# Grouped-query attention over a KV cache: K and P transposed in 32x32 word blocks on VectorE, V loaded by 16 KB rows, q and P as block-diagonal weights of four heads

## The chip, the cores and the metric

One core of a Trainium2 chip runs the kernel. The metric is the device time of one execution in microseconds, the median of several. The span in a profile (first to last instruction) is about 1.9 us shorter than that time. PE is TensorE (PEld its weight loads), DVE is VectorE, ACT is ScalarE, POOL is GpSimd, SP issues the DMAs. A number after PV, V or K is the batch (0 to 31). The trace holds 16 landing events for each load (a load is one DMA); "landed" below means the last of them, and all times are us from the start of the span.

## The reference, cut to what matters

```python
B, Sq, D = 32, 4, 1024
Hq, Hkv, Sk, Dh = 32, 4, 2048, 128          # all bfloat16
q = (x @ wq)                                # [32 batches, 4 tokens, 32 heads, 128]
k = repeat(k_cache, 8); v = repeat(v_cache, 8)
scores = einsum("bhqd,bhkd->bhqk", q, k) * Dh ** -0.5
o = einsum("bhqk,bhkd->bhqd", softmax(scores), v)
return o @ wo
```

Each batch has 2 MB of K and 2 MB of V: 134.2 MB in all. wq and wo are 8.4 MB each. A batch's 4 KV heads (the groups g) serve 8 query heads of 4 tokens each, so 32 rows of scores per group and 128 per batch. "QK" below is the scores, "PV" the product of the probabilities P with V, and the "projection" is the product with wo at the end.

## The kernel before

Each operation is recorded with the names of what it waits for, and each engine has a list of its own. In each turn of the loop the kernel computes the scores of batch i, transposes K of batch i+1, and does PV for batch i-2. K comes by rows of 16 KB (64 tokens of 256 bytes), V by rows of 4 KB:

```python
R = 32; T = Sk // R; C = 4; TV = T // C; TT = TV // 2; NKB = 3; NVB = 3
WO = (8, 8, 8, 5, 2, 1)                     # heads of wo in each load
def load_k(b):                              # 64 tokens to a partition: 16 KB rows
    ... K_sb[:, b % NKB, :, :], k_cache[b].rearrange("g (r t) d -> (g r) t d", r=R) ...
def load_v(b):                              # 16 tokens of each group to a partition: 4 KB rows
    src = v_cache[b].rearrange("g (p t) d -> p g (t d)", p=128)
    dst = V_sb[:, b % NVB, :, :, :].rearrange("p g t d -> p g (t d)")
```

K and P are transposed on TensorE as 32-bit words (two bfloat16 each) into PSUM and copied out by DVE and ACT. QK and PV use parts of the array, each group in its own columns:

```python
def pe_fill(b, f):                          # 8 times a batch, 4 transposes each
    ... e.transpose(buf..., words(K_sb[:, b % NKB, t:t + 2, :]...), identf[:, :]) ...
def pv_mm(buf, i, g, t, waits, done):       # 64 times a batch
    ... e.matmul(buf[32 * g:32 * (g + 1), 0:Dh], lhsT=pt(i, t, g), rhs=V_sb[:, i % NVB, g, t, :],
                 start=(t == 0), stop=(t == TV - 1), tile_position=(0, 32 * g)) ...
```

After the loop come the last PVs and the projection (`oproj`): 32 heads, two matmuls of 512 columns each, waiting for each chunk of wo and for the output of the last batch.

## Time and profile before

| | before |
|---|---|
| time, median | 379.7 us |
| span | 377.8 us |
| DMA rate, 4 to 24 us (16 KB rows only) | 430 GB/s |
| DMA rate, 100 to 300 us (K by 16 KB, V by 4 KB rows) | 417 GB/s |
| PE / DVE / ACT / POOL busy | 70 / 56 / 45 / 0 % |

From the page of the kernel before: the busy share of each engine, the DMA share in tenths and the GB/s in 40 slices of 9.4 us, the chain of waits that ended last (by engine), and three groups (line, engine, operation, tiles, shapes, count, busy us and mean ns of one, idle before and its cause).

```profile
PE 264.8 (70%) x4553; PEld 190.7 (50%) x3953; DVE 213.0 (56%) x299; ACT 169.9 (45%) x266; POOL 1.3 (0%) x9
...
DMA  8999999999999999999999999999999999999982
GB/s 333 427 434 427 414 409 417 416 417 418 419 423 419 415 421 418 416 414 419 415 416 418 416 416 418 418 419 419 417 418 416 414 419 414 413 405 375 373 331 80
...
DMA 70%; PE 15%; DVE 5%; ACT 5%; SPq 3%; issue 1%
...
L264 PE MATMUL ps_r<-identf,K_sb 128*128 128x128 f32 x1024 | 122.9, 277 | 44.1 <-DMA K_sb<-in_k_cache_dram 41.3
L317 PE MATMUL ps_r<-V_sb,PT_sb 128*32 128x128 bf16 x2048 | 35.5, 222 | 44.6 <-DMA V_sb<-in_v_cache_dram 40.6
L355 ACT ACTIVATE P_sb<-ps_s,negmx 128x2048 bf16<-128x2048 f32 x32 | 63.3, 1979 | 7.0 <-DVE negmx L351 7.0
```

The DMA line is full from start to end, no engine is, and what PE waits for is K and V. The slices step from 427 to 434 GB/s (wq and K) down to about 417 once V joins. The DMA view of two stretches of the same run says it in one number each (packets, MB, rate, and how many packets are small): the first stretch is 4 to 24 us, the second 100 to 300 us.

```profile
DMA packets 589, 8.60 MB, mean 430 GB/s; under 512 B 64, under 2 KB 64, under 8 KB 64
...
DMA packets 13326, 83.43 MB, mean 417 GB/s; under 512 B 632, under 2 KB 632, under 8 KB 10767
```

The end of the timeline before (start us, duration us, engine, line, operation) shows a short tail behind the last V:

```profile
344.60 1.08 PE L317 MATMUL ps_r<-V_sb,PT_sb 128*32 128x128 bf16 x64 [1.48 <-DMA V_sb<-in_v_cache_dram]
...
350.30 1.90 PE L317 MATMUL ps_r<-V_sb,PT_sb 128*32 128x128 bf16 x64 [3.84 <-DMA V_sb<-in_v_cache_dram]
...
356.86 0.65 PE L368 MATMUL ps_s<-w_sb,QT_sb 128*128 128x512 bf16 x1 [3.90 <-DMA w_sb<-in_wo_dram]
```

PV takes 1.08 us where the granted clock was 1.00 (V 30, at 344.6 us) and 1.90 us where it was 0.50 (V 31), and starts the moment its V lands: V 31 at 350.3 us. The projection begins soon after and then waits for wo.

### The profile page before, as it was taken

To read this page: it belongs to the slowest core of one execution; us is meant where nothing else is said; L and a number is where in the kernel's file an instruction comes from. 1 tells how busy PE (TensorE), PEld (TensorE's weight loads), DVE (VectorE), ACT (ScalarE), POOL (GpSimd) and SP (SyncE) were. 2 spreads that over 40 slices of the span, in tenths; PEclk is the share of its full clock that TensorE was granted. 3 is DMA by queue.
4 is the path that set the end of the run, shared out by engine and by line. 5 is a ranking of instruction groups with operands and counts; after the bars stand their busy time and mean duration, and the time that the engine had idled before them with its cause. 6 is when DMAs were issued, how large, how long until landed. Compare 5 with 4: busy or idle time off the path is not lost.

```text
span 377.8 us, 9230 instructions
## 1 busy us (share of the span) xinstructions
PE 264.8 (70%) x4553; PEld 190.7 (50%) x3953; DVE 213.0 (56%) x299; ACT 169.9 (45%) x266; POOL 1.3 (0%) x9
## 2 busy tenths in 40 slices
PE   1889888887777666777656677766667666663476
PEld 0018656665557555555535555555545555542222
DVE  0026886777664666666656666666666666661000
ACT  1025565555555555544435554555544444444100
POOL 1000000000000000000000000000000000000000
PEclk9999999999998999999999999999999999999599
DMA  8999999999999999999999999999999999999982
GB/s 333 427 434 427 414 409 417 416 417 418 419 423 419 415 421 418 416 414 419 415 416 418 416 416 418 418 419 419 417 418 416 414 419 414 413 405 375 373 331 80
DMA packets 26774, 152.11 MB, mean 403 GB/s; under 512 B 1264, under 2 KB 1520, under 8 KB 22128
## 3 DMA queue, kind: packets, MB, share of 16 engines
q1 hardware_dynamic: 26592, 151.39, 98.2%
q8 instruction: 33, 0.54, 0.6%
q10 hardware_dynamic: 144, 0.13, 0.1%
q14 instruction: 5, 0.04, 0.0%
HBM read 151.26 MB, written 0.26 MB: 401 GB/s over the span
## 4 chain that ended last, share of the span: by engine, by line
DMA 70%; PE 15%; DVE 5%; ACT 5%; SPq 3%; issue 1%
DMA V_sb<-in_v_cache_dram 52%; DMA K_sb<-in_k_cache_dram 7%; DMA w_sb<-in_wo_dram 6%; DMA w_sb<-in_wq_dram 5%; DVE mx L350 4%; ACT P_sb L355 4%; PE ps_r L317 3%; PE ps_r L282 3%; SPq L175 3%; PE ps_r L264 2%; PE ps_s L16 2%; PE ps_s L308 2%; PE ps_s L237 1%; PE ps_s L368 1%; ACT KT_sb L276 1%
## 5 line engine op out<-in xcount | busy, mean ns | idle before, releaser
L264 PE MATMUL ps_r<-identf,K_sb 128*128 128x128 f32 x1024 | 122.9, 277 | 44.1 <-DMA K_sb<-in_k_cache_dram 41.3
L264 PEld LDWEIGHTS ps_r<-identf,K_sb 128*128 128x128 f32 x1024 | 112.7, 142 | 52.2 <-DMA K_sb<-in_k_cache_dram 44.6
L274 DVE COPY KT_sb<-ps_r 128x512 f32<-128x512 f32 x128 | 84.9, 688 | 30.9 <-PE ps_r L264 30.0
L276 ACT COPY KT_sb<-ps_r 128x512 f32<-128x512 f32 x128 | 69.6, 599 | 48.1 <-PE ps_r L264 48.1
L289 DVE COPY PT_sb<-ps_r 128x512 f32<-128x512 f32 x64 | 41.3, 687 | 65.2 <-PE ps_r L282 65.2
L350 DVE TENSOR_REDUCE mx<-ps_s 128x1 f32<-128x2048 f32 x32 | 73.3, 2292 | 7.0 <-PE ps_s L16 7.0
L317 PE MATMUL ps_r<-V_sb,PT_sb 128*32 128x128 bf16 x2048 | 35.5, 222 | 44.6 <-DMA V_sb<-in_v_cache_dram 40.6
L355 ACT ACTIVATE P_sb<-ps_s,negmx 128x2048 bf16<-128x2048 f32 x32 | 63.3, 1979 | 7.0 <-DVE negmx L351 7.0
L317 PEld LDWEIGHTS ps_r<-V_sb,PT_sb 128*32 128x32 bf16 x2048 | 30.4, 98 | 51.4 <-ACT KT_sb L276 43.1
L344 ACT ACTIVATE QT_sb<-ps_r 128x128 bf16<-128x128 bf16 x32 | 23.7, 739 | 55.0 <-PE ps_r L340 55.0
L282 PE MATMUL ps_r<-identf,P_sb 128*128 128x128 f32 x256 | 34.9, 279 | 2.6 <-ACT KT_sb L276 1.4
L334 ACT ACTIVATE o_sb<-ps_r,rinv 128x128 bf16<-128x128 f32 x32 | 11.8, 368 | 48.2 <-PE ps_r L317 48.2
L282 PEld LDWEIGHTS ps_r<-identf,P_sb 128*128 128x128 f32 x256 | 27.4, 141 | 6.3 <-ACT KT_sb L276 1.9
L308 PE MATMUL ps_s<-KT_sb,QT_sb 64*32 64x512 bf16 x512 | 26.5, 390 | 0.9 <-DVE KT_sb L274 0.9
L16 PE MATMUL ps_s<-KT_sb,QT_sb 64*32 64x512 bf16 x512 | 26.1, 383 | 0.0
L376 DVE CAST y_sb<-ps_s 128x512 bf16<-128x512 f32 x1 | 0.7, 692 | 30.5 <-PE ps_s L368 30.5
L368 PE MATMUL ps_s<-w_sb,QT_sb 128*128 128x512 bf16 x32 | 13.1, 409 | 5.9 <-DMA w_sb<-in_wo_dram 5.9
L340 PEld LDWEIGHTS ps_r<-ident,o_sb 128*128 128x128 bf16 x32 | 3.1, 96 | 20.9 <-issue 20.1
L368 PEld LDWEIGHTS ps_s<-w_sb,QT_sb 128*128 128x128 bf16 x32 | 4.9, 154 | 16.3 <-issue 8.4
L16 PE MATMUL ps_s<-w_sb,QT_sb 128*128 128x512 bf16 x32 | 12.9, 403 | 0.0
L223 DVE CAST KT_sb<-ps_r 128x512 bf16<-128x512 f32 x2 | 1.3, 687 | 20.1 <-PE ps_r L209 20.1
L308 PEld LDWEIGHTS ps_s<-KT_sb,QT_sb 64*32 64x32 bf16 x512 | 7.4, 90 | 10.4 <-issue 5.2
(28 smaller groups left out, 66.0 us busy)
## 6 DMA issues: line engine op xcount, KB each, us to landing
K_sb<-in_k_cache_dram SPq DMA_DIRECT2D x32, 2048.0 KB, 26.3
V_sb<-in_v_cache_dram SPq DMA_DIRECT2D x32, 2048.0 KB, 27.4
w_sb<-in_wq_dram SPq DMA_DIRECT2D x4, 2048.0 KB, 14.0
w_sb<-in_wo_dram SPq DMA_DIRECT2D x2, 2048.0 KB, 22.9
w_sb<-in_wo_dram SPq DMA_DIRECT2D x1, 1792.0 KB, 20.0
w_sb<-in_wo_dram SPq DMA_DIRECT2D x1, 1280.0 KB, 18.6
w_sb<-in_wo_dram SPq DMA_DIRECT2D x1, 512.0 KB, 14.9
P_sb<-in_x_dram SPq DMA_DIRECT2D x1, 256.0 KB, 2.7
```

The lines of the kernel that those rows point to most:

```text
L16: return eng.add_instruction(mybir.InstMatmult(name=nc.get_next_instruction_name(), engine=eng.engine, start_tensor_calc=start, stop_tenso ...
L264: p.op("pe", lambda e, c=c, t=t: e.transpose(buf.rearrange("p (n c) -> p n c", c=C)[:, :, c], words(K_sb[:, b % NKB, t:t + 2, :].rearrange ...
L274: p.op("dve", lambda e: e.tensor_copy(dst, buf), waits, ("kt", b, f))
L276: p.op("act", lambda e: e.copy(dst, buf), waits, ("kt", b, f))
L282: p.op("pe", lambda e, q=q: e.transpose(buf[:, q * 128:(q + 1) * 128], words(P_sb[:, (4 * f + q) * 256:(4 * f + q + 1) * 256]), identf[:, :]),
L289: p.op("dve", lambda e: e.tensor_copy(dst, buf), [("ptf", i, f)] + ([("pv", i - 2)] if i > 1 else []), ("pt", i, f))
L308: mm = lambda e, a=(out, lhsT, rhs), w=w, pos=(DW * par, 32 * g): e.matmul(a[0], lhsT=a[1], rhs=a[2], start=(w == 0), stop=(w == 1), tile_ ...
L317: p.op("pe", lambda e: e.matmul(buf[32 * g:32 * (g + 1), 0:Dh], lhsT=pt(i, t, g), rhs=V_sb[:, i % NVB, g, t, :], start=(t == 0), stop=(t = ...
L344: p.op("act", lambda e: e.activation(oT_sb[:, i * Sq:(i + 1) * Sq, 0:Hq].rearrange("p s h -> p h s"), buf[:, 0:128].rearrange("p (h s) -> ...
L350: p.op("dve", lambda e: e.tensor_reduce(mx[:, i % 4:i % 4 + 1], ps_s[:, :], AX.X, ALU.max), [("qk", i)], ("mx", i))
L355: p.op("act", lambda e: e.activation(P_sb[:, :].rearrange("p (n a) -> p n a", a=2), ps_s[:, :].rearrange("p (a n) -> p n a", a=2), ACT.Exp ...
L368: mm = lambda e, a=(out, lhsT, rhs), h=h: e.matmul(a[0], lhsT=a[1], rhs=a[2], start=(h == 0), stop=(h == Hq - 1), skip_group_check=True)
```

## The change

The intent is a DMA stream of 16 KB rows only, and fewer operations on TensorE. K and V are both laid out with 64 tokens of one group on each partition, so V's rows are 16 KB too. DVE transposes K and P directly in SBUF, in blocks of 32x32 words. Partition 32g+r then belongs to group g alone. So q and P are written into block-diagonal weights (group g's 32 partitions and 32 columns, zeros elsewhere), and one matmul over the full array does all four groups. GpSimd writes the blocks. Eight slots of 2 MB hold K, V, wq and wo in turn. The core of the diff:

```diff
-        src = v_cache[b].rearrange("g (p t) d -> p g (t d)", p=128)
+        src = (k_cache if kind == "k" else v_cache)[b].rearrange("g (r t) d -> (g r) t d", r=R)
+        p.dma("sp", lambda e, s=s, src=src: e.dma_start(big[:, s, :, :], src), waits, (kind, b), f"s_b{s}")
...
-    WO = (8, 8, 8, 5, 2, 1)
+    WO = (4, 4, 4, 4, 4, 4, 4, 2, 1, 1)
...
+        def kt(i, chunks):                       # four a batch, 128x1024 words each
+            ... p.op("dve", lambda e, s=src, d=dst: e.transpose(d, s), waits, ("kt", i, c))
+        def pt(i):
+            p.op("dve", lambda e: e.transpose(dst, src), [("exp", i)] + ([("pd", i - 2)] if i > 1 else []), ("pt", i))
+        def pd(i):                               # P into the diagonal: one buffer, PD_sb
+            for g in range(G):
+                src = words(PT_sb[rows, i % 2, :, :, :]...)
+                dst = words(PD_sb[rows, :, g, :, :]...)
+                p.op("pool", lambda e, s=src, d=dst: e.tensor_copy(d, s),
+                     (["pd0", ("pt", i)] + ([("pv", i - 1)] if i else [])) if g == 0 else [], ...)
+        def pe_pv(i):
+            for t in range(T):                   # 64 matmuls of the full array
+                ... e.matmul(buf[:, 0:Dh], lhsT=PD_sb[:, t // 2, :, :, t % 2]..., rhs=big[:, slot_of["v", i], t, :],
+                             start=(t == 0), stop=(t == T - 1)),
+                    waits + [("pd", i), ("v", i)] if t == 0 else [], ...
...                                              # after the loop
+        pe_pv(L - 1); o_evac(L - 1); pd(L); pe_ot(L - 1); ot_evac(L - 1); pe_pv(L); ...
```

Note in `pd` that the copy of batch i waits for PV of batch i-1, since there is one buffer.

## The prediction

> **What bounds the kernel now.** DMA. The span is 377.8 us; the page shows 152.1 MB at 403 GB/s, and its slices hold 414 to 423 GB/s with DMA at 9 from start to wo. The chain of waits is 70% DMA. PE is busy 70%, DVE 56%, ACT 45%, POOL 0%. The DMA view by window gives 430 GB/s while only 16 KB rows move (wq and K, 4 to 36 us), 417 once V's 4 KB rows take turns with K (100 to 300 us), and 379 for wo. At 417 one batch (4.19 MB) takes 10.06 us, at 430 it takes 9.75. In the timeline the last matmuls run 3.7 us behind the last wo landing.
>
> **What the change does.**
> - V comes by 16 KB rows: 134.2 MB of K and V at 430 instead of mostly 417 saves about 9.5 us of DMA time.
> - It removes 32 K transposes (3.7 us of PE) and 8 P transposes (1.1 us) a batch, and 10 PSUM evacuations of 0.6 to 0.7 us on DVE and ACT. None bounds.
> - DVE gets five word transposes of 128x1024 a batch.[...] max reads 2048 words in 2.29 us here: estimate 1.14 us each. DVE: 5 x 1.14 + 2.29 + 0.3 = 8.3 us a batch.
> - PE: QK is 16 full matmuls of 512 columns, 0.216 us apart in the trace's output projection: 3.5 us. PV is 64 pairs of weight load and matmul of 128 columns.[...]
> - POOL copies P into the diagonal: four copies of 1024 words. Memsets of 1 and 128 elements take 98 and 204 ns here, a cast of 128 takes 289: estimate 0.85 ns a word plus 0.2 us, with hand-over 1.15 us each, 4.6 us a batch.
>
> **The critical path.** The diagonal P has one buffer, so PV(i), copy(i+1), PV(i+1) is a loop[...]. So the middle stays DMA bound at about 430 GB/s, V 29 landing near 327 us. But the tail becomes serial: PV 29, copy, PV 30, copy, PV 31 take some 26 us, then 32 heads of output projection at 0.43 us (13.8 us), then 3.3 us of output. That ends near 371 us, while DMA is done near 360. Half of the gain is lost there. With 1.9 us between span and time: 373 us.
>
> **Chances.** 8 in 10 between 363 and 398. Faster by over 2%: 0.44; within 2%: 0.31; slower: 0.25.
>
> **What would show it.** Right: mid slices at 427 to 432 GB/s; DVE transposes of 1.1 to 1.2 us; POOL copies of 1.0 to 1.2 us, POOL busy near 50%;[...] 10 us or more between last wo landing and end. Wrong: PV waiting for POOL in every batch and mid slices below 420.
>
> **What would make it wrong.** Loop PV plus copy over 9.75 us: each 0.1 us over costs about 3 us. Word transposes at half rate (DVE 14 us a batch, about 500 us total). POOL copies at 1.5 ns a word. Weight loads not hidden behind PV.[...]

The loop came to 9.2 us: 4.6 for the copies, 0.4 for the hand-over, and the term for PV; it was set against the 9.75 us of DMA a batch. The 26 us of the tail, and with them the sum of 373 us, hold that term too.

## The result, and the profile after

| | before | after |
|---|---|---|
| time, median (range, runs) | 379.74 us (379.60 to 379.82, 4) | 379.47 us (378.45 to 379.89, 4) |
| ratio, 95% interval | | 0.999 (0.997 to 1.001) |
| span | 377.8 us | 378.1 us |
| DMA rate, 100 to 300 us | 417 GB/s | 427 GB/s |
| last PV ends | 352.2 us | 359.4 us |
| last load (of wo) landed | 372.6 us | 362.1 us |
| projection done, its copy out starts | 374.5 us | 374.8 us |

A ratio here is the mean time of one kernel's fast runs over that of the other's fast runs of the same rounds, so it is not quite the ratio of the medians. The result is right. The time is the same; 373 us was forecast.

The same lines of the page after the change, with the groups that are new:

```profile
PE 284.5 (75%) x2741; PEld 149.6 (40%) x2272; DVE 272.4 (72%) x270; ACT 119.9 (32%) x134; POOL 166.7 (44%) x265
...
DMA  8999999999999999999999999999999999999900
GB/s 333 433 426 432 428 428 430 426 432 420 427 423 426 432 423 431 425 426 430 423 433 421 427 429 419 435 419 432 426 426 430 423 432 423 432 401 386 358 34 28
...
DMA 33%; PE 32%; DVE 15%; ACT 7%; issue 7%; POOL 4%; SPq 1%; POOLq 0%
...
L308 POOL COPY PD_sb<-PT_sb 32x1024 f32<-32x1024 f32 x128 | 132.3, 1034 | 144.1 <-DVE KT_sb L267 66.5
L267 DVE STREAM_TRANSPOSE KT_sb<-big 128x1024 f32<-128x1024 f32 x128 | 150.7, 1216 | 6.1 <-DMA big<-in_k_cache_dram 6.0
L315 PE MATMUL ps_r<-big,PD_sb 128*128 128x128 bf16 x2048 | 130.6, 229 | 32.2 <-DMA big<-in_v_cache_dram 22.2
L292 ACT ACTIVATE P_sb<-ps_s,negmx 128x2048 bf16<-128x2048 f32 x32 | 81.6, 2550 | 82.9 <-DVE negmx L288 82.9
L300 DVE STREAM_TRANSPOSE PT_sb<-P_sb 128x1024 f32<-128x1024 f32 x32 | 39.8, 1245 | 14.6 <-ACT P_sb L292 14.6
```

The stream did become faster: about 427 in the slices where 417 stood. And it ends earlier: the slice with 358 GB/s (349.7 to 359.2 us) is the last full one, and the two last show 34 and 28 GB/s, where before still had 331 in its last but one. The last load landed at 362.1 us, so 16 us pass between the end of the loads and the end of the kernel (5 us before), and the chain is now 33% DMA, not 70%. The gain is there; it is lost after the loads.

The timeline of the tail after the change, cut to PV (L315), the copies into the diagonal (L308) and the copy out of the last batch (L332):

```profile
316.29 5.36 PE L315 MATMUL ps_r<-big,PD_sb 128*128 128x128 bf16 x64 [3.81 <-DMA big<-in_v_cache_dram]
...
321.77 4.32 POOL L308 COPY PD_sb<-PT_sb 32x1024 f32<-32x1024 f32 x4 [7.21 <-PE ps_r L315]
...
326.14 3.75 PE L315 MATMUL ps_r<-big,PD_sb 128*128 128x128 bf16 x64 [0.98 <-POOL PD_sb L308]
...
330.02 4.32 POOL L308 COPY PD_sb<-PT_sb 32x1024 f32<-32x1024 f32 x4 [2.77 <-DVE KT_sb L267]
...
334.39 3.75 PE L315 MATMUL ps_r<-big,PD_sb 128*128 128x128 bf16 x64 [0.29 <-POOL PD_sb L308]
...
338.26 4.32 POOL L308 COPY PD_sb<-PT_sb 32x1024 f32<-32x1024 f32 x4 [3.93 <-PE ps_r L315]
...
342.64 6.25 PE L315 MATMUL ps_r<-big,PD_sb 128*128 128x128 bf16 x64 [2.92 <-POOL PD_sb L308]
...
349.01 4.32 POOL L308 COPY PD_sb<-PT_sb 32x1024 f32<-32x1024 f32 x4 [6.43 <-PE ps_r L315]
...
353.38 6.01 PE L315 MATMUL ps_r<-big,PD_sb 128*128 128x128 bf16 x64 [3.81 <-POOL PD_sb L308]
...
360.12 0.72 ACT L332 ACTIVATE QT_sb<-ps_r 128x128 bf16<-128x128 bf16 x1 [0.32 <-PE ps_r L328]
```

PV 27, at 316.29, waits for its V and runs 5.36 us (the granted clock was 0.50 from 318 to 320 us and 0.68 over the whole of it). From there on PV and copy alternate without overlap: each copy starts 0.1 us after the PV before it ended, each PV when its copy is done. V 28 to V 31 landed at 325.9, 330.9, 335.7 and 340.6 us, while PV 28 to PV 31 started at 326.1, 334.4, 342.6 and 353.4: only PV 28 starts near the landing of its V. At the end there are no K loads between the Vs, so Vs land every 5 us (2.1 MB at 427 GB/s), while the alternation takes 3.75 + 4.37 + 0.13 = 8.25 us a batch. And the last two PVs take 6.25 and 6.01 us instead of 3.75. Then follow 13.8 us of projection, from 361.0 us to its copy out at 374.8.

The windows view of the tail, before and then after (start and end of the stretch, its length, then busy us and count for PE, PEld, DVE, ACT and POOL, the granted clock, the DMA share and GB/s), shows the clock and the early end of the loads:

```profile
345.00:355.00 10.00, 3.08 (x116) 2.36 (x102) 0.00 (x0) 2.21 (x4) 0.00 (x0) 0.72 1.04 371
355.00:365.00 10.00, 7.69 (x29) 2.33 (x15) 0.00 (x0) 0.00 (x0) 0.00 (x0) 0.77 1.03 378
365.00:378.00 13.00, 8.10 (x37) 2.60 (x17) 0.69 (x1) 0.60 (x1) 0.00 (x0) 1.00 0.33 123
```

```profile
345.00:355.00 10.00, 5.73 (x61) 5.42 (x60) 0.00 (x0) 1.09 (x2) 4.13 (x4) 0.67 1.05 387
355.00:365.00 10.00, 8.39 (x70) 5.69 (x60) 0.00 (x0) 1.09 (x2) 0.00 (x0) 0.84 0.45 167
365.00:378.00 13.00, 9.94 (x46) 3.17 (x22) 0.69 (x1) 0.60 (x1) 0.00 (x0) 1.00 0.06 20
```

The clock fell while TensorE waited. It had done one small transpose in 4.5 us of waiting for the copy (338.14 to 342.64) when PV 30 started; the granted clock was 1.00 until 341 us and 0.50 from 342 to 347 us (windows of 1 us), and PV 30 took 1.67 times as long. The fall came about 3 us after PV 29 ended, with the transpose in between. Ahead of PV 31 it was the same: 4.5 us of waiting with one transpose (348.89 to 353.38), and a granted clock of 0.50 from 352 to 358 us. What sets the time of the fall was not tested.

### The profile page after: what moved, and what is told of

Same layout as the page of the kernel before. It is cut to its first block, busy times and chain, and to the rows that moved or that the text cites. A ratio compares the mean times of both kernels' runs of the same rounds, so it can differ in the third digit from the quotient of the medians.

```text
span 378.1 us, 5957 instructions
## 1 busy us (share of the span) xinstructions
PE 284.5 (75%) x2741; PEld 149.6 (40%) x2272; DVE 272.4 (72%) x270; ACT 119.9 (32%) x134; POOL 166.7 (44%) x265
## 4 chain that ended last, share of the span: by engine, by line
DMA 33%; PE 32%; DVE 15%; ACT 7%; issue 7%; POOL 4%; SPq 1%; POOLq 0%
DMA big<-in_v_cache_dram 28%; PE ps_s L16 16%; DVE mx L287 11%; PE ps_r L315 9%; ACT P_sb L292 7%; DMA big<-in_wq_dram 5%; PE ps_s L279 5%; POOL PD_sb L308 4%; DVE KT_sb L267 2%; PE ps_s L343 2%; DVE negmx L288 1%; DVE QT_sb L240 1%; DVE KT_sb L224 1%; SPq L154 0%; POOLq L110 0%
## 5 line engine op out<-in xcount | busy, mean ns | idle before, releaser
L308 POOL COPY PD_sb<-PT_sb 32x1024 f32<-32x1024 f32 x128 | 132.3, 1034 | 144.1 <-DVE KT_sb L267 66.5
L267 DVE STREAM_TRANSPOSE KT_sb<-big 128x1024 f32<-128x1024 f32 x128 | 150.7, 1216 | 6.1 <-DMA big<-in_k_cache_dram 6.0
L315 PE MATMUL ps_r<-big,PD_sb 128*128 128x128 bf16 x2048 | 130.6, 229 | 32.2 <-DMA big<-in_v_cache_dram 22.2
L315 PEld LDWEIGHTS ps_r<-big,PD_sb 128*128 128x128 bf16 x2048 | 126.2, 103 | 39.7 <-POOL QD_sb L258 20.0
L16 PE MATMUL ps_s<-KT_sb,QD_sb 128*128 128x512 bf16 x384 | 108.2, 390 | 0.0
L292 ACT ACTIVATE P_sb<-ps_s,negmx 128x2048 bf16<-128x2048 f32 x32 | 81.6, 2550 | 82.9 <-DVE negmx L288 82.9
L279 PE MATMUL ps_s<-KT_sb,QD_sb 128*128 128x512 bf16 x128 | 50.1, 392 | 44.6 <-ACT P_sb L292 38.6
L279 PEld LDWEIGHTS ps_s<-KT_sb,QD_sb 128*128 128x128 bf16 x128 | 12.7, 99 | 123.9 <-issue 74.1
L332 ACT ACTIVATE QT_sb<-ps_r 128x128 bf16<-128x128 bf16 x32 | 23.5, 735 | 102.0 <-PE ps_r L328 102.0
L300 DVE STREAM_TRANSPOSE PT_sb<-P_sb 128x1024 f32<-128x1024 f32 x32 | 39.8, 1245 | 14.6 <-ACT P_sb L292 14.6
L258 POOL COPY QD_sb<-QT_sb 32x64 f32<-32x64 f32 x128 | 29.4, 230 | 41.6 <-DVE QT_sb L240 25.4
L16 PE MATMUL ps_s<-big,QT_sb 128*128 128x512 bf16 x32 | 12.1, 379 | 1.2 <-ACT QT_sb L332 1.1
L343 PE MATMUL ps_s<-big,QT_sb 128*128 128x512 bf16 x30 | 11.4, 379 | 0.0
```

Source lines behind the costliest of these rows:

```text
L16: return eng.add_instruction(mybir.InstMatmult(name=nc.get_next_instruction_name(), engine=eng.engine, start_tensor_calc=start, stop_tenso ...
L258: p.op("pool", lambda e, s=src, d=dst: e.tensor_copy(d, s), waits if g == 0 else [], ("qd", i) if g == G - 1 else None)
L267: p.op("dve", lambda e, s=src, d=dst: e.transpose(d, s), waits, ("kt", i, c))
L279: mm = lambda e, a_=(out_, lhsT, rhs), f=first, l=last: e.matmul(a_[0], lhsT=a_[1], rhs=a_[2], start=f, stop=l, skip_group_check=True)
L292: p.op("act", lambda e: e.activation(P_sb[:, :, :, :].rearrange("p t r w -> p t w r"), ps_s[:, :].rearrange("p (t w r) -> p t w r", w=2, r=R),
L300: p.op("dve", lambda e: e.transpose(dst, src), [("exp", i)] + ([("pd", i - 2)] if i > 1 else []), ("pt", i))
```

## The experiments

Theory A: 16 KB rows give about 7 us through the middle, and the tail takes them back, because PV and the diagonal copy alternate on one buffer. Rival B: the tail is long because projection and output follow everything. Rival C: it is the clock of TensorE. And it had to be shown that the rate comes from the rows, not from the eight slots or the order of loads. Ratios are against the kernel before on the same chip.

| run | what | median us | ratio (95%) |
|---|---|---|---|
| e1_halves | after, copy and PV handed over in halves | 369.89 | 0.974 (0.973 to 0.976) |
| e2_warm | after, extra matmuls ahead of PV 30 and 31 | 376.26 | 0.991 (0.988 to 0.993) |
| e3_before_v16 | before, V by 16 KB rows (wrong on purpose) | 372.90 | 0.982 (0.981 to 0.984) |
| e4_v4 | after, V by 4 KB rows | 387.59 | 1.021 (1.020 to 1.023) |
| e5_before_wo | before, wo in the new chunks | 378.80 | 0.998 (0.996 to 0.999) |
| e6_halves_v4 | e1_halves, V by 4 KB rows | 377.19 | 0.993 (0.991 to 0.995) |
| e7_tail_dve | e1_halves, last two copies on VectorE | 368.67 | 0.971 (0.970 to 0.973) |
| e8_warm_all | e7_tail_dve, extra matmuls ahead of PV 20 to 31 | 371.78 | 0.979 (0.978 to 0.980) |
| e9_warm_mid | the same, ahead of PV 20 to 28 only | 368.38 | 0.970 (0.968 to 0.971) |
| after_again | after, unaltered | 380.08 | 0.999 (0.997 to 1.002) |

### e1_halves: the alternation taken apart

```diff
+    NP = 2
         def pd(i):
-            for g in range(G):
-                ... all 32 word rows of group g, waiting for ("pv", i - 1)
+            for m in range(NP):
+                ts = slice(T // 2 // NP * m, T // 2 // NP * (m + 1))
+                for g in range(G):
+                    ... rows ts of group g, waiting for ("pv", i - 1, m); done ("pd", i, m)
         def pe_pv(i):
-                    waits + [("pd", i), ("v", i)] if t == 0 else [], ("pv", i) if t == T - 1 else None)
+                    (waits + [("v", i)] if t == 0 else []) + [("pd", i, t // (T // NP))],
+                    ("pv", i, t // (T // NP)) if (t + 1) % (T // NP) == 0 else None)
```

A second buffer would have been the plainest experiment, but SBUF is too full for one: the build stops with the message that the second buffer needs 16384 bytes a partition and that 10080 are left.

> The changed kernel, with the diagonal copy of P and PV each handed over in two halves, so that the copy of the next batch starts when PV has read the first half. Nothing else moves; the copies are 8 of 512 words instead of 4 of 1024. Theory A (the gain of the faster DMA is lost in the tail, where PV 27, copy, PV 28, copy ... PV 31 run one after the other while all V but the last few have landed): the last PV ends near 349 instead of 359.4 us, the output projection is then bound by the landing of wo (near 358.5) and the span ends near 364: 365 us, range 362 to 369. Rival B (the tail is long because the output projection of 13.5 us and the output follow everything): PV ends earlier but at most 2 us are won: 377 to 380 us. Rival C (the clock of TensorE alone: two PV of 6.2 us at half clock): the wait for the copy is gone, but PV 30 and PV 31 stay at 6 us: near 373 us.

The time is 369.89 us, 9.6 us under the changed kernel. PV 28 starts at 326.14 us in both traces; the gain comes after it. In the timeline the two halves of PV 30 and PV 31 now fit between halves of the copy, and the clock stays up (the granted clock was 1.00 from 340 to 350 us):

```profile
339.81 1.95 PE L320 MATMUL ps_r<-big,PD_sb 128*128 128x128 bf16 x32
...
341.95 1.96 PE L320 MATMUL ps_r<-big,PD_sb 128*128 128x128 bf16 x32 [0.20 <-POOL PD_sb L311]
342.05 5.38 POOL L311 COPY PD_sb<-PT_sb 32x512 f32<-32x512 f32 x8 [0.16 <-POOL PD_sb L311]
...
344.81 1.95 PE L320 MATMUL ps_r<-big,PD_sb 128*128 128x128 bf16 x32 [0.22 <-POOL PD_sb L311]
...
347.48 1.96 PE L320 MATMUL ps_r<-big,PD_sb 128*128 128x128 bf16 x32 [0.72 <-POOL PD_sb L311]
```

The last PV ends at 349.4 us instead of 359.4, as theory A said. Rival B, at most 2 us, falls. Rival C expected PV 30 and 31 to stay slow; they did not, and TensorE's longest wait between PV 29 and PV 31 is 1.8 us there. But A's figure for the whole, 365 us and at most 369, was missed by 0.9 us: it took the projection as bound by the landing of wo, while in the trace it starts at 351.0 us and runs 13.8 us without a wait for DMA. The end is the last PV plus 1.6, 13.8 and 3.3 us.

### e2_warm: the clock alone

```diff
+        pe_warm(10)       # matmuls of 512 columns into an unused part of the scores' PSUM
         pe_pv(L - 1)
...
+        pe_warm(15)
         pe_pv(L)
```

> The changed kernel, with 10 and 15 matmuls without use ahead of PV 30 and PV 31, in the time in which TensorE waits for the diagonal copy. It separates the clock from the serial chain. If the half clock of the last two PV is a cost of its own on the chain, both fall from 6.2 and 6.0 us to about 3.8 and the time falls by 3 to 5 us, to 375 to 376.5 us. If the chain is bound by something else, or the extra matmuls delay PV, the time stays at 379.5 us or rises.

The timeline of the last three PVs, with the extra matmuls (L360) in between:

```profile
336.25 3.75 PE L316 MATMUL ps_r<-big,PD_sb 128*128 128x128 bf16 x64 [0.98 <-POOL PD_sb L309]
...
340.74 2.33 PE L360 MATMUL ps_s<-KT_sb,ident 128*128 128x512 bf16 x10
...
344.51 3.75 PE L316 MATMUL ps_r<-big,PD_sb 128*128 128x128 bf16 x64 [1.44 <-POOL PD_sb L309]
...
352.76 3.75 PE L316 MATMUL ps_r<-big,PD_sb 128*128 128x128 bf16 x64 [0.57 <-POOL PD_sb L309]
```

Both fell to 3.75 us, the time that PV 28 and 29 took in the trace after at a granted clock of 1.00. From the start of PV 29 to the end of PV 31 it is 20.3 us instead of 25.0, so 4.7 us of the tail were the clock; of the 10.0 us by which e1_halves brought the last PV forward, the other 5.3 are, by subtraction, the overlap. The time fell by 3.2 us (by 2.9 between the two profiled runs, where PV 29 itself started 1.9 us later). The clock is thus a part of the loss, and itself a consequence of the alternation; e1_halves won it back too without any extra work.

### e3_before_v16 and e4_v4: the rows alone, in both kernels

```diff
 # e3, on the kernel before (tokens of V no longer match P: a wrong result)
-            src = v_cache[b].rearrange("g (p t) d -> p g (t d)", p=128)
-            dst = V_sb[:, b % NVB, :, :, :].rearrange("p g t d -> p g (t d)")
+            src = v_cache[b].rearrange("g (r t) d -> (g r) (t d)", r=R)
+            dst = V_sb[:, b % NVB, :, :, :].rearrange("p g t d -> p (g t d)")
 # e4, on the changed kernel (result right)
+                for m in range(4):
+                    ts = slice(16 * m, 16 * (m + 1))
+                    p.dma("sp", ... e.dma_start(big[:, s, ts, :], src[:, ts, :]), ...)
```

> The kernel before, with V loaded by 16 KB rows and nothing else changed (the result is wrong on purpose: the tokens of V no longer match P). Theory A (the kernel before is DMA bound through the middle and its tail follows the last load): middle at 427 GB/s instead of 417, each of some 30 batches 0.24 us shorter: 7 us less, 372 to 373 us. Rival (row size does not set the rate; the deeper ring of buffers or the order of the loads does): 379.7 us and 417 GB/s.

> The changed kernel with V loaded by 4 KB rows, as four DMAs of 512 KB for each V, into the same places; the result stays right. Theory A: the middle falls from 427 to 417 GB/s and V 27 lands 6 to 7 us later; the serial tail hangs on V 27, so the whole loss shows: 386 us, range 384 to 388. If the tail were not tied to the landing of V, or the rate did not come from the rows, it stays within 2 us of 379.5.

The DMA view of 100 to 300 us, first of e3_before_v16 and then of e4_v4:

```profile
DMA packets 5850, 85.22 MB, mean 426 GB/s; under 512 B 648, under 2 KB 648, under 8 KB 648
```

```profile
DMA packets 14355, 83.53 MB, mean 418 GB/s; under 512 B 1593, under 2 KB 1593, under 8 KB 11809
```

Both came as expected: e3_before_v16 is 6.7 us faster than the kernel before, with the same instructions on PE, DVE, ACT and POOL; e4_v4 is about 8 us slower than the changed kernel. The rate follows the rows in either kernel. It also says where the result went: the kernel before with the faster stream is at 373 us (that this is also the figure forecast for the changed kernel is chance), and the changed kernel has the faster stream and stands at 379.5. e3 is not a version to use: in the layout of before, a partition holds tokens of all four groups, and 16 KB rows do not fit that; this is why the change brings block-diagonal weights at all. One caution on e4: it has four times as many DMAs of a quarter of the size, so rows and number of DMAs change together there; e3 changes the rows alone.

### e6_halves_v4: are the rows still worth it with the short tail?

The diffs of e1_halves and e4_v4 together.

> The kernel of e1_halves with V by 4 KB rows (four DMAs of 512 KB for each V). Says what the 16 KB rows are worth once the tail is short: the middle at 417 to 418 GB/s instead of 427, the last V lands 7 to 8 us later, and the tail still hangs on V and P: 377 to 378 us. Rival (with the tail mended, wo and the projection bind and the rows no longer matter): below 373 us.

377.19 us, 7.3 us over e1_halves. With the tail mended the whole gain of the rows reaches the end.

### e5_before_wo: the chunks of wo

```diff
-    WO = (8, 8, 8, 5, 2, 1)
+    WO = (4, 4, 4, 4, 4, 4, 4, 2, 1, 1)
```

> The kernel before, with wo in the chunks of the changed kernel (4 heads each, then 2, 1, 1) and nothing else. In the trace of before the projection had caught up with wo at 365.6 us, waited for a chunk of 8 heads until 367.5, and then ran 16 heads back to back to 374.5. If the chunks make it wait, 4 heads arrive at a time and it ends about 1 us after the last landing: 2.5 to 3.5 us less, 376 to 377 us. If the DMA ring or the landing order sets it, 379.5 us.

Only 0.9 us came. In this run the seventh chunk of four heads landed at 370.6 us, and the last three chunks (2, 1 and 1 heads) at 371.9, 372.6 and 373.2 us, each before TensorE had come to it. So 8 heads ran back to back, until 374.2 us:

```profile
368.08 0.46 PE L368 MATMUL ps_s<-w_sb,QT_sb 128*128 128x512 bf16 x1 [0.69 <-DMA w_sb<-in_wo_dram]
...
370.67 0.45 PE L368 MATMUL ps_s<-w_sb,QT_sb 128*128 128x512 bf16 x1 [0.62 <-DMA w_sb<-in_wo_dram]
...
374.18 0.69 DVE L376 CAST y_sb<-ps_s 128x512 bf16<-128x512 f32 x1 [29.24 <-PE ps_s L368]
```

The projection thus ended 1.0 us after the last landing, as expected, and 1.9 us after it in the kernel before (374.5 and 372.6 us). But the last landing itself was no earlier: 373.2 us. Behind it there was 1.9 us to win from and not 3.7, so the expected 2.5 to 3.5 us could not come.

### e7, e8 and e9: a version that beats both

After e1_halves the end hangs on the last PV. e7_tail_dve puts the copies of the last two batches on VectorE, which has nothing to do there:

```diff
-                    p.op("pool", lambda e, s=src, d=dst: e.tensor_copy(d, s),
+                    p.op("dve" if i >= L - 1 else "pool", lambda e, s=src, d=dst: e.tensor_copy(d, s),
```

(with the copy of batch 30 recorded ahead of the P transpose of batch 31).

> The kernel of e1_halves, with the diagonal copies of the last two batches (30 and 31) on VectorE, which is idle there, instead of GpSimd. In e1_halves the last PV ended at 349.45 us and the end came 18.7 us later (1.6 us to the first matmul of the output projection, 13.8 us of projection, 3.3 us of output), so a shorter chain before the last PV should show whole at the end until the landing of wo, near 358.5 us plus 4.5, binds. If a VectorE copy of 512 words takes 0.4 to 0.6 us, the last PV ends 3 to 4 us earlier: 366 to 367 us. If VectorE copies are no faster than the 0.65 us a copy on GpSimd, 1 us or less is won: 369 us.

The copies did become faster, eight in 3.45 us against 5.38:

```profile
342.92 3.45 DVE L311 COPY PD_sb<-PT_sb 32x512 f32<-32x512 f32 x8 [0.39 <-PE ps_r L320]
```

But the last PV ended at 348.9 us, only 0.5 us earlier. In this run PV 27, waiting for its V, ran 6.48 us (5.37 us in e1_halves; the granted clock was 0.77 on average from 310 to 320 us), and everything behind it on TensorE came about 1 us later. 368.67 us is 1.2 us better than e1_halves, where 3 us had been expected.

e8_warm_all is to keep the clock up, with 32 matmuls of 128 columns ahead of each PV from batch 20 on.

> The kernel of e7_tail_dve with 32 matmuls of 128 columns without use ahead of each PV from batch 20 on, in the time in which TensorE waits for V, so that the clock stays up. In e7_tail_dve PV 27 ran at half clock (6.48 us instead of 3.74) and held QK 30 and the softmax of the last batches behind it. If that cold PV is on the tail's chain, the last PV ends 1.5 to 3 us earlier than 348.9 and the time is 366 to 367.3 us. If the landing of K 31 and V sets the chain, or the extra matmuls delay PV, 368.7 us or more.

It missed: 371.78 us. PV 27 took 3.75 us, and the granted clock was 1.00 from 300 to 360 us, but in the last three batches TensorE does not wait for V, and there each set of extra matmuls stands in the way for 1.95 us. e9_warm_mid leaves those three out:

> As e8_warm_all, but with the extra matmuls only ahead of PV 20 to 28, not ahead of the last three, where TensorE does not wait for V and the trace of e8_warm_all shows them delaying each PV by 1.95 us. With PV 27 warm, QK 30 started at 320.4 instead of about 323 us; if the rest follows, the last PV ends near 346.5 us (348.9 in e7_tail_dve) and the time is 366 to 367 us. If the landing of K 31 and V 28 eats the gain, 368 to 369 us.

The last PV now ends at 346.95 us, as expected, 2 us earlier than in e7_tail_dve, but the time is 368.38 us: nearly nothing more. Now the landing of wo binds:

```profile
348.55 0.41 PE L354 MATMUL ps_s<-big,QT_sb 128*128 128x512 bf16 x1 [0.91 <-ACT QT_sb L343]
...
359.72 0.45 PE L354 MATMUL ps_s<-big,QT_sb 128*128 128x512 bf16 x1 [0.61 <-DMA big<-in_wo_dram]
...
361.30 0.14 PEld L354 LDWEIGHTS ps_s<-big,QT_sb 128*128 128x128 bf16 x1 [0.29 <-DMA big<-in_wo_dram]
```

The intervals of e7_tail_dve and e9_warm_mid overlap, so the simpler e7_tail_dve is the version to keep: 2.9% faster than the kernel before. What is left is the stream itself and, in the trace of e7_tail_dve, the 18.7 us from the end of the last PV to the end (348.9 to 367.6 us).

> The changed kernel again, unaltered, on the same chip as e9_warm_mid, as a control: 378.5 to 380 us.

The control, after_again, came at 380.08 us (378.29 to 381.18), ratio 0.999 again. Its runs scatter more than those of the kernel before. In its trace PV 28 had waited for its V until 326.04 us and itself took 5.02 us (3.75 in the trace after), so which PVs are slow differs from run to run.

## Why the prediction was wrong

It forecast 1.8% less time and nothing came. The mechanism was the right one; the tail was sized too small.

- **DMA bounds the kernel before: right.** e3_before_v16 changed nothing but the rows and won 6.7 us.
- **16 KB rows, 430 instead of 417 GB/s, 9.5 us: mostly right.** Measured were 427 GB/s and 6.7 to 8.1 us (e3, e4 and e6). The difference between 430 and 427 is 134.2 MB / 427 less 134.2 MB / 430, about 2.2 us.
- **Costs of the new operations: right, as far as they stand.** PV 3.75 us at a granted clock of 1.00, 59 ns for each of its 64 pairs of weight load and matmul, POOL copies 1.03 us (1.15 with hand-over; measured 1.09 from start to start), the loop of PV and copy 8.25 us (9.2). By the copies of 64 words (230 ns) and of 1024 (1034 ns), a copy on POOL took 0.84 ns a word and some 0.18 us besides. The word transposes on DVE took 1.22 us (K) and 1.25 us (P), 7 to 9% more than the 1.14 estimated from max. The middle stayed DMA bound, as forecast. Not foreseen: exp rose from 1.98 to 2.55 us, and the chain on the page after does pass through it (7%, "ACT"); no run tested what it costs.
- **"Half of the gain is lost there": this step failed.** All of it was lost. The text has the serial part start with the landing of V 29 near 327 us and take 26 us to the end of PV 31 near 353. In the trace PV 31 ended at 359.4, 6.4 us later; the 18.7 us from there to the end were as forecast (the sum there was about 18). The mis-sized term is the start: PV 29 started at 334.4, 7.4 us late. Of these, 3.9 are the landing, since V 29 landed at 330.9 and not at 327. The other 3.5 are the wait for the copy: the alternation did not begin with PV 29 but with PV 27, and PV 28 and one more copy stood in between.
- **The 26 us held by luck.** Measured are 25.0 us from the start of PV 29 to the end of PV 31. But the forecast's own costs, two loops of 9.2 and one PV, came to 22.6; with the clock up it is 20.3 (e2_warm). The low clock of PV 30 and 31, which the forecast did not have, added 4.7, and the margin in the 26 hid it.
- **Why V 28 and V 29 landed late.** The slices after sum to 136.4 MB by 321.4 us (34 slices of 9.45 us), and everything up to and including V 28 is 136.6 MB (x 0.3, wq 8.4, 61 loads of 2.1). Yet it landed at 325.9. The trace shows why a count of bytes is too early: the 16 landing events of V 28 lie between 321.2 and 325.9 us, those of V 29 between 326.1 and 330.9; those of V 26 lie 3.4 us apart. The count gives about the first event, and PV waits for the last, 4.7 us later. What sets the events so far apart was not tested.
- **"The last matmuls run 3.7 us behind the last wo landing": a wrong reading.** That is where the last visible wait for wo ended (370.8 us). The last wo landed at 372.6 and the matmuls ended at 374.5, 1.9 us behind. e5_before_wo showed finer chunks to be worth 0.9 us.
- **The range** of 363 to 398 us held, and "PV waiting for POOL in every batch and mid slices below 420" did not appear in the middle: from 100 to 300 us PV waited 15.8 us for V and 2.0 us for POOL, and single slices of 419 stand beside 429 to 435, with a mean of 427. The sign that did appear was named: "10 us or more between last wo landing and end". It was 16.

## What to carry to other kernels

When a stream of loads bounds the middle of a kernel, count what still has to run after the last load of each kind has landed, buffer by buffer: here a hand-over on one buffer, 8.25 us a turn, was free while Vs came every 10 us and became the critical path when they came every 5 us. Take as the landing of a load its last event and not the time at which the bytes add up: here they were 4 to 5 us apart. Hand over in halves before asking for a second buffer: here it cost eight short copies instead of four and won 9.6 us. And look at the clock in a serial tail on TensorE: here it cost twice, since after the waits of 4.5 us the granted clock stood at 0.50, and PV took 6.25 and 6.01 us instead of 3.75.
